# A spectral and GeGLU network in FP32: rows mixed at the loads for a norm, not at residual rows and sequence matrices

## The chip, the cores and the metric

One core of one Trainium2 chip runs the whole program. The time is device microseconds per execution; the profiled execution is one of them, with every instruction and DMA packet recorded. A run of the kernel before took 1851.21 us (median of 3, 1846.16 to 1852.52).

## The reference

Four layers on x of 2048 rows by 512 columns, in FP32: a Fourier mixing layer, a GeGLU layer, and both again, each on the normalised x and added to x.

```python
def _A_ref(x, dft_seq_re, dft_seq_im, dft_hid_re, dft_hid_im):
    a = jnp.einsum("bsd,ed->bse", x, dft_hid_re)
    b = jnp.einsum("bsd,ed->bse", x, dft_hid_im)
    return jnp.einsum("ts,bse->bte", dft_seq_re, a) - jnp.einsum("ts,bse->bte", dft_seq_im, b)

def _B_ref(x, w_gate, w_up, w_down):
    return (_gelu(x @ w_gate) * (x @ w_up)) @ w_down

x = A_x
x = x + _A_ref(_layernorm(x), A_dft_seq_re, A_dft_seq_im, A_dft_hid_re, A_dft_hid_im)
x = x + _B_ref(_layernorm(x), B_w_gate, B_w_up, B_w_down)
```

The two last lines run twice, with the same matrices; the layers are numbered 0 to 3 here.

## The kernel before, in words

**Precision and products.** Every FP32 operand is split into a high part (ACT, `split`, L113) and a low part (DVE, L114), and a product is three matmuls (`mm3`, L147 to L149). Large products are formed by a Strassen-like scheme with seven block products, whose names (A11, A12, S1 to S4, T1 to T4) are those of its blocks and of sums of blocks.

**Tiles.** x stands in DRAM in groups of 512 rows (`xs[layer, g]`, four groups), four tiles of 128 rows in a group. Nearly all tiles in SBUF are 128 by 512 and come from one pool of 98 slots (`sb`, named s). All loads are issued by SP's queue in the order in which they stand; most stores by POOL's.

**Mixing layers (0 and 2, `mix`).** The matrices of the sequence transform (`ws`, 128 tiles of 128 by 512) are loaded as a stream of items (`load_next`, L220), split, and multiplied with the normalised rows; then the matrices of the hidden transform (`wh`) follow. `plan` (L324) gives the order of the steps for the four blocks b: A11 and A12 for the first FORE blocks (four in layer 0, two in layer 2), then for each block S2, S3, A22 and the three groups of the hidden transform. A tile is loaded up to RAW items ahead of its split, and split up to AHEAD items ahead of its use. At the end of a block `x_add` (L175) adds the product to x and stores four tiles. Beside the products a queue of small steps runs, one after each tile's six matmuls (`step`): norms and preparations for what comes.

**GeGLU layers (1 and 3, `geglu`).** A layer is done in two halves (w = 0 and 1) of two parts of 512 rows each. `block_steps` (L502) prepares a half: eight norms (`normed`, L439), each of one tile of 128 rows, each transposed in blocks of 32 by 32 on DVE (L515) into a wide tile; one wide tile of 1 MB for each part goes to DRAM (L518) and comes back in pieces of 32 rows (L529), which completes the transpose. The products with gate, up and down weights (`wb`, `wd`) follow. `load_rows` loads x for the sum and `add_rows` adds and stores.

**What "mixed" is.** The transpose by 32-row blocks leaves the rows of a group in another order: with n the tile, j the block of 32 rows in a tile and t the row in a block, row (n, j, t) stands at place (j, n, t). All products of the layer come out in that order. So before the change tile i of the sum holds 32 rows of each of the four tiles of its group, and x is loaded and stored for it by one transfer of four blocks of 32 rows:

```python
        if mixed:
            return xs[layer, g].rearrange("(n j t) d -> j n t d", n=NT, t=32)[n]
```

The four tiles of the last group of layer 1 stay in SBUF (`fresh`) for layer 2, in mixed order; so in layer 2 the sequence matrices' tiles that meet them, k from 12 to 15 of 16, are put together from four row blocks too (`seq_tile`, L341):

```python
        if layer and k >= NS - NT:
            return ws[(n + 1) * NS - NT:(n + 1) * NS, (k % NT) * 32:(k % NT + 1) * 32]
```

A scheduler that simulates the engines sets the order of instructions on each engine, so an edit in one place moves independent instructions in others.

Of the kernel before, what the change touches and what calls it, by code (L numbers as in the profile page):

```python
# [14 lines left out]
P = 128  # L15
S, D, F = 2048, 512, 1792
NS = S // P
# [4 lines left out]
NT = TB // P  # L22
# [17 lines left out]
def fnet_geglu(ctx: ExitStack, tc: tile.TileContext, x_in, ws, wh, wgu, wdn, out):  # L40
# [27 lines left out]
    nc = tc.nc  # L68
# [37 lines left out]
    sb = Slots(slots, "s", NSLOT)  # L106
# [30 lines left out]
    def plus(out, a, b):  # L137
        nc.vector.tensor_tensor(out, a, b, op=ALU.add)  # L138
# [12 lines left out]
    half = slice(0, 256), slice(256, 512)  # L151

    xg = x_in.rearrange("(g r) d -> g r d", r=TB)
    og = out.rearrange("(g r) d -> g r d", r=TB)
    xs = {(0, g): xg[g] for g in range(NB)}
# [3 lines left out]
    xs.update({(4, g): og[g] for g in range(NB)})  # L161
    fresh = {}

    def rows(layer, i, mixed=False):
        g, n = divmod(i, NT)
        if mixed:
            return xs[layer, g].rearrange("(n j t) d -> j n t d", n=NT, t=32)[n]
        return xs[layer, g][n * P:(n + 1) * P]

    def x_load(layer, i, mixed=False):  # L170
        t = sb.get()
        nc.sync.dma_start(t, rows(layer, i, mixed))
        return t

    def x_add(layer, i, t, ps, mixed=False, keep=False, engine=nc.gpsimd):  # L175

        plus(t, t, ps)
        ps8.put(ps)
        engine.dma_start(rows(layer + 1, i, mixed), t)  # L179
        if keep:  # L180
            fresh[i] = t
        else:
            sb.put(t)
# [81 lines left out]
    def make_a11(k):  # L265

        def run(v):
            held[k] = v
            return split_slot(v)
        return run  # L270
# [42 lines left out]
    def skewed():  # L313

        order = []
        for k in range(NK + SKEW):
            order += [(0, k)] if k < NK else []
            order += [(1, k - SKEW)] if k >= SKEW else []
        return order
# [17 lines left out]
    def bare(layer, b, what):  # L337

        return layer == 0 and b == 0 and what == "A11"

    def seq_tile(layer, n, k):  # L341

        if layer and k >= NS - NT:
            return ws[(n + 1) * NS - NT:(n + 1) * NS, (k % NT) * 32:(k % NT + 1) * 32]
        return ws[n * NS + k]

    def mix_items(layer):
        def raw(make, *tiles):
            items.append((F32, tiles, make, None))

        for b, what in plan(layer):
            tiles = [[seq_tile(layer, b * 2 + m, k) for k in range(NS)] for m in range(2)]
            (a11, a12), (a21, a22) = ((r[:NK], r[NK:]) for r in tiles)
            hold = b >= FORE[layer]
            if what == "A11":
                for k in range(NK):
                    raw(as_is if bare(layer, b, what) else make_a11(k) if hold else plain, a11[k])
            elif what == "A12":
                for t in a12:
                    raw(plain, t)  # L360
            elif what == "S2":
                for second, k in skewed():
                    if second:
                        raw(make_s1(k))
                    else:
                        raw(make_s2(k), a21[k], a22[k], *(() if hold else (a11[k],)))
            elif what == "S3":
                for second, k in skewed():
                    if second:
                        raw(make_s4(k), a12[k])  # L370
                    else:
                        raw(make_s3(k))
            elif what == "A22":
                for t in a22:
                    raw(plain, t)
            else:
                for m, c in what:
                    if layer == 0 and b == 0:
                        items.append((F32, (wh[m * ND + c],), make_hid_first(m, c), (m, c)))
                    else:  # L380
                        items.append((F32R, halves(whs[m, c]), make_hid(m, c), (m, c)))
# [20 lines left out]

    known = {}

    def row_of(layer, i):
        x = fresh.pop(i, None)
        return x_load(layer, i) if x is None else x

# [27 lines left out]
        known[layer, i] = norm_terms(layer, i, x, junk)  # L436
        sb.put(x, junk)

    def normed(layer, i):  # L439
        x = row_of(layer, i)  # L440
        z = sb.get()
        rstd, shift = known.pop((layer, i), None) or norm_terms(layer, i, x, z)
        nc.scalar.activation(z, x, AF.Identity, bias=shift, scale=rstd)  # L443
        sb.put(x)
        return z
# [56 lines left out]
    def block_steps(layer, w):  # L502

        zt, t, wide = {}, {}, {}
        turned = [dram.tile([P, NT * D], F32, name=f"t{layer}_{w}_{part}") for part in range(2)]

        def norm(i):

            def run():
                z = normed(layer, w * 2 * NT + i)  # L510
                part, n = divmod(i, NT)
                if n == 0:
                    wide[part] = tpool.tile([P, NT * D], F32, name="wide")
                to = wide[part].rearrange("p (b n t) -> p b n t", n=NT, t=32)
                nc.vector.transpose(to[:, :, n], z.rearrange("p (b t) -> p b t", t=32))  # L515
                sb.put(z)
                if n == NT - 1:
                    nc.gpsimd.dma_start(turned[part], wide.pop(part))  # L518
            return run

        def fetch(c):

            def run():
                for part in range(2):
                    v = zt[c, part] = sb.get()
                    for i in range(P // 32):
                        cols = turned[part][:, (c * 4 + i) * P:(c * 4 + i + 1) * P]
                        to = v[i * 32:(i + 1) * 32]
                        nc.sync.dma_start(  # L529
                            to.rearrange("p (j t) -> p j t", t=P), cols.rearrange("(j p) t -> p j t", p=32)  # L530
                        )
            return run

        def difference(a, b):
            v = sb.get()
            minus(v, a, b)
            return v

        def first(c):
            def run():  # L540
                v = t[f"B{1 + c // 2}1", c % 2] = zt.pop((c, 0))
                blocks[f"B{1 + c // 2}1", c % 2] = split_slot(v)
            return run

        def second(c):
            def run():
                v = zt.pop((c, 1))
                if c < 2:
                    t["B12", c] = v
                    t["T1", c] = difference(v, t["B11", c])  # L550
                    sb.put(t.pop(("B11", c)))
                else:
                    c0 = c - 2
                    t["T2", c0] = difference(v, t["T1", c0])
                    t["T3", c0] = difference(v, t["B12", c0])
                    sb.put(t.pop(("B12", c0)))
                    blocks["B22", c0] = split_slot(v)
                    sb.put(v)
            return run

        def fourth(c):
            def run():
                t["T4", c] = difference(t["B21", c], t["T2", c])
                sb.put(t.pop(("B21", c)))
            return run

        def divide(name, c):
            def run():
                blocks[name, c] = split_slot(t[name, c])
                sb.put(t.pop((name, c)))  # L570
            return run

        one = [norm(i) for i in range(2 * NT)]
        two = [fetch(c) for c in range(ND)] + [first(c) for c in range(ND)] + [second(c) for c in range(ND)]
        two += [fourth(c) for c in range(2)]
        two += [divide(name, c) for name in ("T2", "T3", "T1", "T4") for c in range(2)]
        return one, two
# [211 lines left out]
    def geglu(w, layer):  # L789

        gs, h, acc = {}, {}, {0: [], 1: []}
# [109 lines left out]
        xrows = []  # L901

        def load_rows(part):
            xrows.extend(x_load(layer, (w * 2 + part) * NT + i, True) for i in range(NT))

        def add_rows(part, keep=False):
            for i in range(NT):
                x_add(layer, (w * 2 + part) * NT + i, xrows.pop(0), acc[part][i], True, keep)

        def last_downs(tail):  # L910

            fs = range(NF - tail, NF)
            vs = [take() for _ in fs]
            for f in fs:
                ready(f, 1)
            for i in range(NT):
                ts = slice(i * P, (i + 1) * P)
                for f, v in zip(fs, vs):
                    hs = h[f, 1]
                    mm3(acc[1][i], (hs[0][:, ts], hs[1][:, ts]), v, f == 0, f == NF - 1)  # L920
                x_add(layer, (w * 2 + 1) * NT + i, xrows.pop(0), acc[1][i], True, engine=nc.sync)

        before_mix = w == 1 and layer < 3
        if before_mix:
# [41 lines left out]
    ps = ps8.get()  # L966
# [81 lines left out]
```

## Time and profile before

| | |
|---|---|
| median of 3 runs | 1851.21 us (1846.16 to 1852.52) |
| profiled execution, its own time | 1846.1 us |
| its span, first to last instruction | 1844.3 us |
| PE busy | 1689.5 us (92%), 7168 matmuls |
| DVE, ACT, POOL busy | 1030.4, 782.1 and 191.9 us |
| DMA | 400.01 MB, mean 217 GB/s |
| mean granted TensorE clock | 0.954 |
| `s<-ws` loads, `s<-x` loads | 432 and 134, 256 KB each |

Busy times of the engines overlap, so they don't add up to the span. PE's busy time holds matmuls at a full and at a reduced clock, so a stretch is better read by the number of matmuls that it got through. The layers follow one another: layer 0 to about 400 us, layer 1 to about 850, layer 2 to about 1350, layer 3 to the end.

### The profile page before, as it was taken

The numbers are of one execution on the slowest core, as the hardware profiler recorded it, in microseconds if no ns is written. First come the engines' busy times: TensorE is split into PE (matmuls) and PEld (weight loads), VectorE is DVE, ScalarE is ACT, GpSimd is POOL, SyncE is SP. The second block draws the span as 40 slices with busy tenths as digits, with TensorE's granted clock in tenths as the row PEclk, the third lists the DMA queues.
The fourth block names the chain that finished last, engine by engine and source line by source line (L and its number), as shares of the span: only waits on it lengthen the run. The fifth ranks groups of instructions, "written<-read, shape, count | busy, mean of one in ns | idle before, by whom it ended". The sixth has DMA issues, their size and how long they took to land.

```text
span 1844.3 us, 22260 instructions
## 1 busy us (share of the span) xinstructions
PE 1689.5 (92%) x7168; PEld 1372.9 (74%) x7168; DVE 1030.4 (56%) x1748; ACT 782.1 (42%) x1504; POOL 191.9 (10%) x344
## 2 busy tenths in 40 slices
PE   9999999999999789999686879779869999979997
PEld 7878888788887568888465667557748888868886
DVE  8997787877664243355574654745752434343340
ACT  8643455455455254345532232543432335433330
POOL 3201011114331110001100000110000000100000
PEclk9999999999999989999788899889979999989999
DMA  9768678798678785576545655457478458785571
GB/s 353 234 212 296 224 239 302 245 329 302 231 249 258 230 289 173 173 239 186 162 150 155 199 157 176 136 168 221 123 222 303 149 181 288 229 285 164 167 233 46
DMA packets 221604, 400.01 MB, mean 217 GB/s; under 512 B 29872, under 2 KB 49840, under 8 KB 220464
## 3 DMA queue, kind: packets, MB, share of 16 engines
q1 hardware_dynamic: 197520, 333.01, 56.6%
q0 software_dynamic: 23968, 65.59, 10.2%
q8 instruction: 56, 0.92, 0.2%
q14 instruction: 60, 0.49, 0.1%
HBM read 331.87 MB, written 66.58 MB: 216 GB/s over the span
## 4 chain that ended last, share of the span: by engine, by line
PE 52%; issue 19%; DMA 17%; DVE 5%; ACT 4%; SPq 1%; POOL 1%; DVEq 0%; ACTq 0%; POOLq 0%
PE p L148 17%; PE p L147 17%; PE p L149 17%; DMA s<-ws 7%; DMA s<-x 5%; DVE s L114 3%; ACT s L113 2%; DMA s<-wd 1%; DMA x<-s 1%; DMA s<-wh 1%; DVE s L135 1%; DVE s L138 1%; ACT s L428 1%; DMA s<-t 1%; SPq L529 1%
## 5 line engine op out<-in xcount | busy, mean ns | idle before, releaser
L147 PE MATMUL p<-s,s 128*128 128x512 f32 x2368 | 919.9, 399 | 109.5 <-ACT s L113 49.6
L148 PE MATMUL p<-s,s 128*128 128x512 f32 x2368 | 940.3, 398 | 33.8 <-DVE s L114 31.2
L149 PE MATMUL p<-s,s 128*128 128x512 f32 x2368 | 924.3, 396 | 0.7 <-DVE s L114 0.7
L113 ACT ACTIVATE s<-s 128x512 fp32r<-128x512 f32 (+1 forms) x782 | 454.6, 617 | 609.8 <-DMA s<-ws 129.4
L114 DVE TENSOR_TENSOR s<-s,s 128x512 fp32r<-128x512 f32 (+1 forms) x782 | 504.2, 675 | 284.3 <-ACT s L113 236.2
L147 PEld LDWEIGHTS p<-s,s 128*128 128x128 f32 x2368 | 454.9, 193 | 217.5 <-ACT s L113 71.9
L148 PEld LDWEIGHTS p<-s,s 128*128 128x128 f32 x2368 | 455.3, 192 | 139.8 <-DVE s L114 41.9
L149 PEld LDWEIGHTS p<-s,s 128*128 128x128 f32 x2368 | 454.0, 192 | 97.2 <-DVE s L114 1.6
L138 DVE TENSOR_TENSOR s<-s,p 128x512 f32<-128x512 f32 x316 | 211.2, 683 | 278.6 <-PE p L149 210.5
L135 DVE TENSOR_TENSOR s<-s,s 128x512 f32<-128x512 f32 (+1 forms) x314 | 185.9, 609 | 90.1 <-DMA s<-ws 42.8
L142 ACT ACTIVATE s<-p 128x512 f32<-128x512 f32 x224 | 129.9, 592 | 161.3 <-PE p L149 153.2
L786 ACT ACTIVATE s<-s 128x512 f32<-128x512 f32 x112 | 70.1, 629 | 122.7 <-DVE s L138 121.8
L138 DVE TENSOR_TENSOR s<-s,s 128x512 f32<-128x512 f32 (+1 forms) x78 | 49.6, 640 | 77.0 <-DMA s<-ws 61.9
L179 POOL DMA_DIRECT2D x<-s x48 | 28.8, 600 | 605.1 <-DVE s L138 604.0
L800 DVE TENSOR_TENSOR s<-s,s 128x512 f32<-128x512 f32 x84 | 57.8, 689 | 2.1 <-ACT s L786 0.3
L429 POOL TENSOR_SCALAR rstd<-rstd 128x1 f32<-128x1 f32 x48 | 14.3, 298 | 425.4 <-ACT s L428 393.6
L443 ACT ACTIVATE s<-s,shift,rstd 128x512 f32<-128x512 f32 x64 | 50.9, 807 | 15.7 <-DMA s<-wd 7.0
L426 ACT ACTIVATE s<-s 128x512 f32<-128x512 f32 x48 | 29.8, 622 | 63.2 <-DMA s<-x 63.1
L207 POOL DMA_DIRECT2D wb<-s x84 | 45.1, 540 | 109.3 <-ACT s L113 88.2
L515 DVE STREAM_TRANSPOSE wide<-s 128x512 f32<-128x512 f32 x32 | 22.2, 704 | 27.7 <-ACT s L443 15.9
L800 DVE TENSOR_TENSOR s<-s,p 128x512 f32<-128x512 f32 x28 | 19.2, 685 | 28.3 <-PE p L149 28.3
L428 ACT ACTIVATE s<-s,mean 128x512 f32<-128x512 f32 x48 | 34.2, 712 | 0.3
(34 smaller groups left out, 244.9 us busy)
## 6 DMA issues: line engine op xcount, KB each, us to landing
s<-ws SPq DMA_DIRECT2D x432, 256.0 KB
s<-wb SPq DMA_DIRECT2D x294, 256.0 KB
s<-wd SPq DMA_DIRECT2D x196, 256.0 KB
s<-x SPq DMA_DIRECT2D x134, 256.0 KB
s<-wh SPq DMA_DIRECT2D x120, 256.0 KB
wb<-s POOLq DMA_DIRECT2D x98, 256.0 KB, 3.8
x<-s POOLq DMA_DIRECT2D x48, 256.0 KB, 6.6
t<-wide POOLq DMA_DIRECT2D x8, 1024.0 KB, 6.8
```

The lines of the kernel that those rows point to most:

```text
L113: nc.scalar.activation(hi, src, AF.Copy)
L114: nc.vector.tensor_tensor(lo, src, f32(hi), op=ALU.subtract)
L135: nc.vector.tensor_tensor(out, a, b, op=ALU.subtract)
L138: nc.vector.tensor_tensor(out, a, b, op=ALU.add)
L142: nc.scalar.activation(v, src, AF.Copy)
L147: nc.tensor.matmul(ps, ah, bh, start=start, stop=False, skip_group_check=True)
L148: nc.tensor.matmul(ps, ah, bl, start=False, stop=False, skip_group_check=True)
L149: nc.tensor.matmul(ps, al, bh, start=False, stop=stop, skip_group_check=True)
L428: nc.scalar.activation(junk, x, AF.Square, bias=mean, accum_out=rstd)
L443: nc.scalar.activation(z, x, AF.Identity, bias=shift, scale=rstd)
L786: nc.scalar.activation(t, g, AF.Gelu_apprx_tanh)
L800: nc.vector.tensor_tensor(t, t, v, op=ALU.mult)
```

## The change

The loads for the norms of the GeGLU layers now take the mixed rows, by four transfers of 32 rows each (`x_load_mixed`), so that the block transpose puts them in their natural order. Everything behind the norm is then in plain order: the residual loads and stores of the GeGLU layers, the fresh tiles, and the sequence matrices' tiles in layer 2. `seq_tile` goes.

```diff
-    def rows(layer, i, mixed=False):
+    def rows(layer, i):
         g, n = divmod(i, NT)
-        if mixed:
-            return xs[layer, g].rearrange("(n j t) d -> j n t d", n=NT, t=32)[n]
         return xs[layer, g][n * P:(n + 1) * P]
...
+    def x_load_mixed(layer, i):
+
+        g, n = divmod(i, NT)
+        t = sb.get()
+        for j in range(NT):
+            r0 = j * P + n * 32
+            nc.sync.dma_start(t[j * 32:(j + 1) * 32], xs[layer, g][r0:r0 + 32])
+        return t
...
-            tiles = [[seq_tile(layer, b * 2 + m, k) for k in range(NS)] for m in range(2)]
+            tiles = [[ws[(b * 2 + m) * NS + k] for k in range(NS)] for m in range(2)]
...
-    def row_of(layer, i):
+    def row_of(layer, i, mixed):
+        if mixed:
+            return x_load_mixed(layer, i)
         x = fresh.pop(i, None)
         return x_load(layer, i) if x is None else x
...
-                z = normed(layer, w * 2 * NT + i)
+                z = normed(layer, w * 2 * NT + i, True)
...
-            xrows.extend(x_load(layer, (w * 2 + part) * NT + i, True) for i in range(NT))
+            xrows.extend(x_load(layer, (w * 2 + part) * NT + i) for i in range(NT))
...
-                x_add(layer, (w * 2 + part) * NT + i, xrows.pop(0), acc[part][i], True, keep)
+                x_add(layer, (w * 2 + part) * NT + i, xrows.pop(0), acc[part][i], keep)
...
-                x_add(layer, (w * 2 + 1) * NT + i, xrows.pop(0), acc[1][i], True, engine=nc.sync)
+                x_add(layer, (w * 2 + 1) * NT + i, xrows.pop(0), acc[1][i], engine=nc.sync)
```

Three places on SP's queue show what moves. A row is a line of the kernel, DMA, the tile written and the tensor read, and the transfer's shape; 128x1x512 is a tile filled from four blocks of 32 rows.

First, layer 2, the last loads of A12 for blocks 0 and 1 and the first of S2. Before:

```order
L220 DMA s_8918<-ws 128x1x512
L220 DMA s_8942<-ws 128x512
L220 DMA s_8960<-ws 128x512
L220 DMA s_8972<-ws 128x512
L220 DMA s_8984<-ws 128x512
L220 DMA s_9008<-ws 128x1x512
L220 DMA s_9020<-ws 128x1x512
L220 DMA s_8906<-ws 128x1x512
L220 DMA s_8890<-ws 128x1x512
L220 DMA s_9032<-ws 128x1x512
L220 DMA s_8930<-ws 128x1x512
L220 DMA s_9044<-ws 128x512
```

Now, at the same place:

```order
L226 DMA s_8966<-ws 128x512
L226 DMA s_8990<-ws 128x512
L226 DMA s_9008<-ws 128x512
L226 DMA s_9020<-ws 128x512
L226 DMA s_9032<-ws 128x512
L226 DMA s_9056<-ws 128x512
L226 DMA s_8938<-ws 128x512
L226 DMA s_9068<-ws 128x512
```

The number and order of the loads are nearly the same, and all have one shape. There are 64 such four-block loads of `ws` in layer 2.

Second, layer 0, block 2, where the norms of layer 1 begin. Before:

```order
L172 DMA s_2862<-x_0_85 128x512
L220 DMA s_2880<-ws 128x512
L220 DMA s_2882<-ws 128x512
L172 DMA s_2907<-x_0_85 128x512
L220 DMA s_2922<-ws 128x512
L220 DMA s_2924<-ws 128x512
L172 DMA s_2951<-x_0_85 128x512
L172 DMA s_2989<-x_0_85 128x512
```

Now:

```order
L178 DMA s_2862<-x_0_85 32x512 x4
L226 DMA s_2883<-ws 128x512
L226 DMA s_2885<-ws 128x512
L178 DMA s_2910<-x_0_85 32x512 x4
L226 DMA s_2928<-ws 128x512
L226 DMA s_2930<-ws 128x512
L178 DMA s_2957<-x_0_85 32x512 x4
L226 DMA s_2932<-ws 128x512
L178 DMA s_2998<-x_0_85 32x512 x4
```

Each norm's load has become four entries, ahead of the same `ws` loads.

Third, the end of the program. Before, the last residual load and the four stores of the last tiles:

```order
L172 DMA s_16040<-x_3_96 128x1x512
L179 DMA out<-s_16040 4x32x512
L179 DMA out<-s_16042 4x32x512
L179 DMA out<-s_16044 4x32x512
L179 DMA out<-s_16046 4x32x512
```

Now:

```order
L169 DMA s_16136<-x_3_96 128x512
L185 DMA out<-s_16136 128x512
L185 DMA out<-s_16138 128x512
L185 DMA out<-s_16140 128x512
L185 DMA out<-s_16142 128x512
```

The order is the same; the four stores have lost their four-block shape.

## Rows read from the trace of the kernel before

**Rows 1.** The page, part 1: busy time of PE, share of span.
```profile
PE 1689.5 (92%) x7168; PEld 1372.9 (74%) x7168; DVE 1030.4 (56%) x1748; ACT 782.1 (42%) x1504; POOL 191.9 (10%) x344
```
**Rows 2.** Windows: stretch, then busy us and instructions of each engine.
```profile
core 0: us, PE busy (x) PEld busy (x) DVE busy (x) ACT busy (x) POOL busy (x), PEclk, DMA share, GB/s
...
50.00:350.00 300.00, 296.05 (x1295) 243.32 (x1294) 251.46 (x425) 143.40 (x272) 37.22 (x61) 0.99 0.76 255
350.00:400.00 50.00, 45.27 (x185) 36.13 (x184) 45.44 (x77) 26.18 (x47) 2.64 (x6) 0.93 0.79 251
...
600.00:700.00 100.00, 80.63 (x325) 64.25 (x324) 37.98 (x60) 41.65 (x93) 12.25 (x25) 0.90 0.79 250
...
850.00:1350.00 500.00, 407.84 (x1642) 324.34 (x1641) 298.10 (x491) 200.90 (x396) 29.96 (x53) 0.90 0.54 164
1350.00:1400.00 50.00, 37.01 (x149) 29.93 (x147) 17.98 (x30) 12.04 (x22) 0.00 (x0) 0.82 0.87 297
1400.00:1600.00 200.00, 200.00 (x884) 165.67 (x883) 75.11 (x115) 81.14 (x162) 12.52 (x26) 1.00 0.68 223
1600.00:1650.00 50.00, 40.16 (x159) 32.16 (x158) 23.16 (x36) 16.61 (x28) 2.85 (x4) 0.90 0.75 224
```
**Rows 3.** Waits of PE, 850 to 1400 us: total, times, longest.
```profile
PE p L147 <- ACT s L113: 35.2, 10, 7.8
PE p L147 <- DVE s L138: 28.5, 2, 14.8
PE p L148 <- DVE s L114: 28.0, 12, 6.7
PE p L147 <- DMA s<-wh: 13.0, 1, 13.0
```
**Rows 4.** Waits of ACT and DVE for ws loads, 50 to 350 us (layer 0).
```profile
ACT s L113 <- DMA s<-ws: 13.6, 13, 2.4
...
DVE s L138 <- DMA s<-ws: 19.8, 9, 3.9
...
DVE s L135 <- DMA s<-ws: 6.9, 8, 1.7
```
**Rows 5.** Waits of ACT and DVE for ws loads, 850 to 1400 us (layer 2).
```profile
ACT s L113 <- DMA s<-ws: 112.8, 31, 9.8
...
DVE s L138 <- DMA s<-ws: 42.1, 11, 8.0
DVE s L135 <- DMA s<-ws: 35.9, 18, 3.7
```
**Rows 6.** Pieces of the chain that ended last: start us, us, what.
```profile
250.24 4.68 DMA s<-x
...
313.97 3.96 DMA s<-ws
...
645.66 2.15 DMA s<-t
...
1092.26 14.69 DMA s<-ws
...
1289.86 10.42 DMA s<-ws
...
1344.92 13.61 DMA s<-wh
...
1612.61 17.37 DMA s<-x
```
**Rows 7.** By tile, SP's issues: duration ns min/median/max, first and last start.
```profile
L220 SPq DMA_DIRECT2D s<-ws x432: 322/374/4064, 1.2 to 1346.5; - x144
...
L529 SPq DMA_DIRECT2D s<-t x128: 302/430/1785, 353.5 to 1610.3; - x128
```
**Rows 8.** SP at the end: its stores by timeline, and its last wait.
```profile
1827.34 8.70 SPq L179 DMA_DIRECT2D out<-s  x4
...
SPq L1044 <- DMA out<-s: 6.9, 3, 3.4
```

More of the change, by code (lines that the diff above doesn't have):

```diff
@@ L162, in fnet_geglu, with x_load, x_add @@
     fresh = {}
-    def rows(layer, i, mixed=False):
+    def rows(layer, i):
         g, n = divmod(i, NT)
-        if mixed:
-            return xs[layer, g].rearrange("(n j t) d -> j n t d", n=NT, t=32)[n]
         return xs[layer, g][n * P:(n + 1) * P]
-    def x_load(layer, i, mixed=False):
+    def x_load(layer, i):
         t = sb.get()
-        nc.sync.dma_start(t, rows(layer, i, mixed))
+        nc.sync.dma_start(t, rows(layer, i))
         return t
-    def x_add(layer, i, t, ps, mixed=False, keep=False, engine=nc.gpsimd):
+    def x_load_mixed(layer, i):
[5 more added lines that the diff above has]
+        return t
+    def x_add(layer, i, t, ps, keep=False, engine=nc.gpsimd):
         plus(t, t, ps)
         ps8.put(ps)
-        engine.dma_start(rows(layer + 1, i, mixed), t)
+        engine.dma_start(rows(layer + 1, i), t)
         if keep:
@@ L339, in bare @@
         return layer == 0 and b == 0 and what == "A11"
[L341 to L345, printed above, removed]
     def mix_items(layer):
@@ L437, in terms_ahead, with normed @@
         sb.put(x, junk)
-    def normed(layer, i):
-        x = row_of(layer, i)
+    def normed(layer, i, mixed=False):
+        x = row_of(layer, i, mixed)
         z = sb.get()
```

## The prediction

> **What bounds the kernel now.** I read the busy times first, then the stretches, then who PE waited for, then who those engines waited for, and last the chain. PE is busy for 92% of the span [rows 1], so it is the bound on average; what can be gained is read from the stretches in which it is not. A stretch is best read by its matmuls. From 1400 to 1600 us PE does 884 in 200 us, 0.2262 us each, with the clock granted in full [rows 2]. Layer 0 from 50 to 350 us does 1295 in 300 us, 0.2317 us each: nearly the same pace. Layer 2 has the same work but does 1642 in 500 us and 149 in the next 50 [rows 2]. At 0.2262 us these 1791 matmuls would take 405 us, so 145 of 550 us are lost there, more than anywhere else. Of these, 105 us are waits of PE for ACT's and DVE's splits and sums and one `wh` load [rows 3], and the other 40 are matmuls at a lower clock: the granted share is 0.90 and 0.82 there against 0.99 in layer 0 [rows 2], part of it at the lower of TensorE's levels (1.2 GHz in place of 2.4), which it falls to after PE has stood still.
>
> Why do ACT and DVE come late? In layer 0 ACT waits 13.6 us in total for `ws` loads, never over 2.4, and DVE 26.7 [rows 4]. In layer 2 ACT waits 112.8 us for them, up to 9.8 at a time, and DVE 78.0 [rows 5]. Yet the DMA engines are less used there: a share of 0.54 and 164 GB/s, against 0.76 and 255 in layer 0 [rows 2]. So it is not the total traffic. In the chain a `ws` load of layer 0 stands with 3.96 us, loads of layer 2 with 10.42 and 14.69, and a `wh` load behind them with 13.61 [rows 6]; SP itself takes up to 4064 ns to issue one `ws` load where the median is 374 [rows 7]. What differs between the layers in these loads is the shape: 64 of layer 2's are put together from four blocks of 32 rows. A load of this shape is slow while the mean DMA share is low, as if few engines carried it, and plain loads issued behind it are slow too.
>
> The Trainium skill has a rule for this (DMA: Bandwidth & Descriptors, "Why a DMA increments its semaphore by 16 and not by 1"): a transfer runs on the largest number of engines up to 16 that divides the outermost sizes of both sides, which is four for four blocks against 128 partitions. By it the change puts these loads on all 16 engines and the sum is the one below; without it the rows only say that this shape and the lateness go together, and the second rival would deserve more. The low share in rows 2 agrees; no row counts engines.
>
> **The change part by part.** The sum is made against the profiled execution, 1846.1 us (span 1844.3 and 1.8 around it); the median of the runs is 5 us above it.
>
> *Sequence matrices, layer 2.* The same 64 loads become plain; nothing else moves on that queue but neighbours that change places. At layer 0's pace 1791 matmuls take 415 us. Both ends of the layer, where the norms before and the weights behind fall in, get what the end of layer 0 lost beyond that pace: 50 us for 185 matmuls, 7.1 us over [rows 2], twice. That makes 429 in place of 550: a gain of 121 us. Bounds: 145 at the pace of rows 2's best stretch; below, no gain at all if the shape is not the cause. I take layer 0 because it is the same code with plain loads, and more loads in the same time (255 GB/s).
>
> *Residual rows of the GeGLU layers.* 32 loads and 32 stores become plain. In the change of halves of layer 3 the chain holds one such load of 17.37 us [rows 6], and 1600 to 1650 us does 159 matmuls, worth 36.0 us: 14.0 lost [rows 2]. I take 10 of them, between 0 and 14. In layer 1 the same place, 600 to 700 us, does 325, worth 73.5: 26.5 lost [rows 2]. But weights are also being made and stored there and all loads crowd, so I take 5, between -8 (the crowd only shifts) and 26.5.
>
> *The last four stores.* They are on the path: the first is issued at 1827.34 us and the fourth 8.70 us later, at about 1836, and SP then waits for their landing [rows 8] until 1844.3. A plain load in a busy stretch lands in about 4 to 5 us [rows 6], so 4 of these 8 us go; between 0 and 6.9.
>
> *Norm loads.* 32 tiles have four entries on SP's queue in place of one. Nearest is the fetch of a transposed piece, also 32 rows: 430 ns an issue against 374 for a plain load [rows 7]. That is 4 times 430 less 374, 1.35 us more for each tile and 43 us of queue in all, ahead of `ws`, `wh`, `wd` and `wb` loads that stand behind them on SP, and ACT waits for four landings. These norms are queued well ahead of their use, and layer 0, where eight of them are made, has waits for `ws` of at most 3.9 us [rows 4]; so the loads that run ahead of PE cover most. Cost between 0 and 43; I take 8, about a fifth, because the cover is thinnest only at the changes of halves. If the cover is gone, the next thing late is the split of the next `ws` tile. The reads now need all four stores of a group instead of one; the group is stored a whole step of the plan earlier, so I cost this at nothing, and what covers it is the block of products in between (if it were late, one landing of 4 to 5 us each half).
>
> Sum: 1846.1 - 121 - 10 - 5 - 4 + 8 = 1714.1 in the profiled execution's terms; the runs lie 0 to 6 above that, so I say **1717 us**.
>
> **The rivals.**
>
> *Layer 2 is also held by something else.* Its plan is not layer 0's: only two blocks have their first half done ahead, so later blocks load, sum and split within the block. For it: PE's longest waits are for DVE sums (14.8 us) and not all of the waits in rows 3 end in a load. Against it: DVE is busy 298 of 500 us there and 251 of 300 in layer 0 [rows 2], so it has room. If half of the 121 stays, the time is 1717 + 60 = 1777.
>
> *The four-block shape is not the cause.* Then layer 2 keeps its 145 us, and what is left is 10 + 5 + 4 - 8 = 11 us: 1838. Were the norm loads also to cost 30 instead of 8, there would be no change. Against it stands the contrast of rows 4 and 5.
>
> *Slower: the pieces serialize.* If the four pieces of a norm's tile land one behind the other, and everything behind them on SP's queue waits with them, each tile costs three more landings. The shortest piece of 32 rows in the chain took 2.15 us [rows 6], so 32 tiles cost 32 x 3 x 2.15 = 206 us if nothing covers it, and with none of the gain in layer 2 this ends at 2050; with it, at about 1717 - 8 + 206 = 1915. It decides from 4.5 us uncovered for each tile, where it eats the 140 us of gain. Against it: 128 such pieces are fetched already, and PE loses 7.1 us where 32 of them go at 350 to 400 us [rows 2]. The Trainium skill speaks for this rival (DMA: Bandwidth & Descriptors, "Rules for kernel authors"): it advises against splitting a tile by partitions, since the parts share the same engines and gain nothing, and wants one transfer of 128 partitions. The rows agree that a piece costs an issue as long as a whole tile's.
>
> **How the numbers follow.** Forecast 0.71; layer 2 held by something else 0.20; shape not the cause 0.05; pieces serialize 0.04. A measurement of this kernel can tell about 0.3% (5.5 us) from no change. Faster 0.94: the first two, and 0.03 of the third; same 0.02, the rest of the third; slower 0.04. The forecast alone, with its bounds, runs from about 1685 to 1760. The range goes on to 1790 to take in the first rival, and leaves the other two and the extreme ends of the bounds out.
>
> **What would show it.** Right: 850 us onward runs at 0.23 to 0.24 us a matmul, the granted clock near 0.98, DMA share near 0.75; ACT's waits for `ws` in layer 2 fall from 112.8 to under 30 us; SP's longest `ws` issue is about 1.5 us; the last store lands within 5 us. Wrong: ACT still waits 60 us or more for `ws` there; or waits for x by the norms (L426, L443) grow by tens of us; or PE waits for transposed pieces at the changes of halves.

## The result and the profile after

The kernel after takes 1695.05 us (median of 4, 1693.33 to 1699.06) against 1851.87 for the kernel before in the same comparison (1846.16 to 1854.31). The ratio is 0.916, with an interval from 0.9132 to 0.9188. The profiled execution has a span of 1691.4 us in place of 1844.3, so 152.9 us have gone.

The page of the kernel after, part 1, with busy time, share of the span and instructions:

```profile
span 1691.4 us, 22376 instructions
PE 1649.1 (98%) x7168; PEld 1350.6 (80%) x7168; DVE 1029.7 (61%) x1748; ACT 784.6 (46%) x1504; POOL 186.1 (11%) x344
```

DVE and ACT do the same work as in [rows 1]; PE is now busy for 98% of the span. PE's busy time fell by 40 us with as many matmuls, because more of them ran at the higher of the clock's two levels: the mean granted share rose from 0.954 to 0.993.

The windows of the kernel after, columns as in [rows 2]. Layer 2 now stands at about 850 to 1250 us:

```profile
50.00:350.00 300.00, 293.52 (x1281) 240.75 (x1280) 248.97 (x420) 142.18 (x270) 35.58 (x59) 0.99 0.76 252
...
600.00:700.00 100.00, 92.04 (x384) 74.66 (x383) 39.31 (x62) 47.52 (x106) 10.70 (x25) 0.95 0.79 260
...
850.00:1250.00 400.00, 388.02 (x1690) 316.92 (x1690) 297.11 (x486) 197.38 (x376) 25.50 (x46) 1.00 0.68 223
```

Layer 2 does 1690 matmuls in 400 us, 0.237 us each, where it did 1642 in 500 [rows 2]. The DMA share rose from 0.54 to 0.68 and the rate from 164 to 223 GB/s: nearly the same bytes in less time. The change of halves of layer 1 does 384 in 100 us in place of 325. Layer 0 is a little slower, 1281 in place of 1295.

The waits of ACT and DVE for `ws` loads in layer 2, 850 to 1245 us, as in [rows 5], and below them all of PE's waits there, as in [rows 3]:

```profile
ACT s L113 <- DMA s<-ws: 21.1, 14, 2.6
...
DVE s L138 <- DMA s<-ws: 16.1, 7, 4.1
...
DVE s L135 <- DMA s<-ws: 6.5, 11, 1.5
```

```profile
PE p L147 <- DMA s<-wh: 4.8, 1, 4.8
PE p L147 <- ACT s L113: 3.6, 3, 1.7
PE p L148 <- DVE s L114: 3.6, 4, 1.5
```

ACT's 112.8 us are 21.1, DVE's 78.0 are 22.6, and PE's 105 us are 12. Where the time went along the program can be read by setting the start of the same matmul, by its count from the first, beside each other in the two traces:

| Matmul number | Place | Before, us | After, us | Difference |
|---|---|---|---|---|
| 1800 | layer 1 begins | 430.2 | 432.6 | +2.4 |
| 2600 | layer 1, before the change of halves | 613.0 | 613.9 | +0.9 |
| 3600 | end of layer 1 | 866.6 | 854.1 | -12.4 |
| 5200 | end of layer 2 | 1374.2 | 1234.1 | -140.0 |
| 6200 | layer 3, change of halves | 1600.8 | 1466.2 | -134.7 |
| 7167 | last matmul | 1834.4 | 1687.1 | -147.3 |

The last 5.6 us lie behind the last matmul: 9.6 us from its end to the span's end before, 3.9 after.

The list of DMA issues of the kernel after, the last number being the median of the us from issue to landing:

```profile
s<-ws SPq DMA_DIRECT2D x432, 256.0 KB, 3.9
...
s<-x SPq DMA_DIRECT2D x102, 256.0 KB, 4.2
...
x<-s POOLq DMA_DIRECT2D x48, 256.0 KB, 4.8
s<-x SPq DMA_DIRECT2D x128, 64.0 KB, 3.6
...
out<-s POOLq DMA_DIRECT2D x12, 256.0 KB, 6.2
...
out<-s SPq DMA_DIRECT2D x4, 256.0 KB, 2.0
```

In the same list of the kernel before, SP's lines have no landing at all, and the stores stand with more:

```profile
s<-ws SPq DMA_DIRECT2D x432, 256.0 KB
...
x<-s POOLq DMA_DIRECT2D x48, 256.0 KB, 6.6
...
out<-s POOLq DMA_DIRECT2D x12, 256.0 KB, 10.3
```

The missing number goes with the shape of the loads. The profile pairs issues and landings only where each transfer leaves 16 completion events on its semaphore. Counted from the trace's semaphore events, a plain load leaves 16, and a load of four blocks that SP issues leaves 5. POOL's stores leave 16 in either shape, so for them the count tells nothing. The runs below show what the count of SP's loads goes with.

SP's own waits for the landing of `ws` loads, which the prediction did not read, show in the same windows. First before (850 to 1400 us), then after (850 to 1245 us):

```profile
SPq L220 <- DMA s<-ws: 52.9, 25, 5.1
```

```profile
SPq L226 <- DMA s<-ws: 2.9, 6, 1.4
```

SP's transfers take turns on eight semaphores, and in the traces of before, after, `e2`, `e3` and `e6` none starts before the one eight places ahead of it has landed; so at most eight are in flight, and a load that lands late also holds back the issue of what stands behind it. This is one way in which lateness and a low DMA share can go together.

### The profile page after: what moved, and what is told of

Same layout as the page of the kernel before. It is cut to its first block, busy times and chain, and to the rows that moved or that the text cites. A ratio compares the mean times of both kernels' runs of the same rounds, so it can differ in the third digit from the quotient of the medians.

```text
span 1691.4 us, 22376 instructions
## 1 busy us (share of the span) xinstructions
PE 1649.1 (98%) x7168; PEld 1350.6 (80%) x7168; DVE 1029.7 (61%) x1748; ACT 784.6 (46%) x1504; POOL 186.1 (11%) x344
## 4 chain that ended last, share of the span: by engine, by line
PE 76%; DMA 9%; DVE 6%; ACT 4%; issue 2%; SPq 2%; POOL 1%; DVEq 0%; ACTq 0%; POOLq 0%
PE p L148 25%; PE p L149 25%; PE p L147 25%; DVE s L114 3%; DMA s<-x 3%; DMA s<-ws 2%; DVE s L135 2%; ACT s L113 2%; DMA s<-wd 1%; SPq L531 1%; DVE s L138 1%; DMA s<-wb 1%; ACT s L445 1%; ACT s L430 1%; ACT s L428 1%
## 5 line engine op out<-in xcount | busy, mean ns | idle before, releaser
L148 PE MATMUL p<-s,s 128*128 128x512 f32 x2368 | 925.6, 391 | 6.4 <-DVE s L114 6.4
L147 PE MATMUL p<-s,s 128*128 128x512 f32 x2368 | 904.5, 393 | 26.5 <-DVE s L138 7.9
L149 PE MATMUL p<-s,s 128*128 128x512 f32 x2368 | 911.8, 391 | 3.5 <-DVE s L114 3.5
L147 PEld LDWEIGHTS p<-s,s 128*128 128x128 f32 x2368 | 446.7, 189 | 127.0 <-ACT s L113 20.7
L148 PEld LDWEIGHTS p<-s,s 128*128 128x128 f32 x2368 | 447.3, 189 | 103.7 <-DVE s L114 10.6
L149 PEld LDWEIGHTS p<-s,s 128*128 128x128 f32 x2368 | 447.0, 189 | 97.7 <-DVE s L114 3.9
```

Source lines behind the costliest of these rows:

```text
L147: nc.tensor.matmul(ps, ah, bh, start=start, stop=False, skip_group_check=True)
L148: nc.tensor.matmul(ps, ah, bl, start=False, stop=False, skip_group_check=True)
L149: nc.tensor.matmul(ps, al, bh, start=False, stop=stop, skip_group_check=True)
```

## The experiments

The theory to test: a transfer whose outermost count is four runs on four DMA engines; it lands late, and what is issued behind it on these engines lands late too. The rivals: layer 2 gains from something else that the plain order brings (stores, schedule); the scatter of rows in DRAM or the split by partitions is what is slow; the four pieces cost more than they save. All ratios are to the kernel before on the same chip. The kernel after, in its own comparison, has 0.916.

**One part alone.** `e1_ws_plain` is the kernel before with this edit:

```diff
-        if layer and k >= NS - NT:
-            return ws[(n + 1) * NS - NT:(n + 1) * NS, (k % NT) * 32:(k % NT + 1) * 32]
         return ws[n * NS + k]
```

> The kernel before, with the 64 four-block loads of the sequence matrices in layer 2 made plain and nothing else (rows of the last group then meet the wrong columns, so layer 2 computes something else at the same cost). If the shape of these loads holds layer 2, it gains what layer 2 gained in the whole change, 127 us: about 1724 us, a ratio of 0.931, with the change of halves in layer 1 and the end as before. If layer 2 gained from the plain order of x, from its stores or from another order of the schedule: under 60 us of gain, 1790 us or more.

It took 1730.15 us, ratio 0.9362 (0.9334 to 0.9391); the span is 1726.4 us, 117.9 below the kernel before. So the shape of 64 loads is worth about 118 us, three quarters of the whole. The first rival falls. The 6 us that are missing to the forecast are not lost in layer 2: by the matmul count, layer 2 gains 122 us, and the change of halves of layer 1, which the edit does not touch, loses 6. ACT's waits for `ws` in layer 2 (850 to 1255 us) show it:

```profile
ACT s L113 <- DMA s<-ws: 25.0, 15, 6.5
```

**The same rows by four transfers.** `e2_ws_pieces` is also the kernel before, reading the same addresses into the same places:

```diff
-            stream["last"] = nc.sync.dma_start(t if dtype == F32 else f32(t), a)
+            if isinstance(a, list):
+                for j, piece in enumerate(a):
+                    stream["last"] = nc.sync.dma_start(t[j * 32:(j + 1) * 32], piece)
+            else:
+                stream["last"] = nc.sync.dma_start(t if dtype == F32 else f32(t), a)
...
-            return ws[(n + 1) * NS - NT:(n + 1) * NS, (k % NT) * 32:(k % NT + 1) * 32]
+            return [ws[(n + 1) * NS - NT + j, (k % NT) * 32:(k % NT + 1) * 32] for j in range(NT)]
```

> The kernel before, with the same 64 tiles read from the same addresses into the same places, but each by four transfers of 32 rows in place of one transfer of four blocks; 192 more entries on SP's queue. If what is slow is the one transfer of four blocks (few engines carry it), most of the 127 us come back: 1725 to 1750 us. If it is the place of the rows in DRAM or the split by partitions that is slow, layer 2 stays as it was or gets worse: 1846 us or more. If pieces are a little worse than plain, the difference to the run with plain loads prices a piece.

It took 1729.2 us, ratio 0.9355 (0.9329 to 0.938), the same as with plain loads, with ACT waiting as little (850 to 1255 us):

```profile
ACT s L113 <- DMA s<-ws: 26.2, 17, 5.1
```

Neither the place of the rows nor the split by partitions is slow; the one transfer of four blocks is. And 192 more entries on SP's queue cost nothing that can be measured here.

**The same part put back.** `e3_ws_blocks` is the kernel after with `seq_tile` as it was before.

> The kernel after, with the four-block loads of the sequence matrices put back in layer 2 alone (it computes something else there). If the shape is the cause in both surroundings, layer 2 loses 120 to 130 us again: 1815 to 1825 us. If the plain residual rows and stores have opened room, it loses clearly less, say 60: 1755 us.

It took 1805.69 us, ratio 0.9768 (0.9743 to 0.9793), 110.9 us of span above the kernel after, all of it between the same two matmuls of layer 2 as above. That is 9 us under the forecast of 120 to 130, but far from the 60 of the rival. ACT in layer 2 (850 to 1355 us) and SP's issues of `ws` (ns min/median/max):

```profile
ACT s L113 <- DMA s<-ws: 104.3, 27, 9.9
```

```profile
L226 SPq DMA_DIRECT2D s<-ws x432: 323/367/3170, 1.2 to 1317.7; - x144
```

The long issues come back with the shape: 3170 ns, where the kernel after has at most 1720.

**Is it the count of blocks?** Two kernels put the 64 loads together from 16 and from 8 blocks, so that the outermost count differs (and with it the number of tiles in DRAM that a load's rows come from). `e9_ws_16`, on the kernel after (`e10_ws_8` has 8 and 16 where this has 16 and 8):

```diff
+    def seq_tile(layer, n, k):
+        if layer and k >= NS - NT:
+            return ws[(n + 1) * NS - 16:(n + 1) * NS, (k % NT) * 8:(k % NT + 1) * 8]
+        return ws[n * NS + k]
...
-            tiles = [[ws[(b * 2 + m) * NS + k] for k in range(NS)] for m in range(2)]
+            tiles = [[seq_tile(layer, b * 2 + m, k) for k in range(NS)] for m in range(2)]
```

> The kernel after, with the same 64 loads of the sequence matrices in layer 2 as one transfer of 16 blocks of 8 rows, from 16 tiles in place of one (other values, the same bytes and rows of 2 KB). If four blocks were slow because the outermost count sets how many DMA engines carry a transfer, 16 blocks are as good as plain: within 5 us of after, 1695 us, where four blocks cost 111. If it is the scatter over several tiles in DRAM or the blocked shape as such, it is slow again: 1780 us or more.

> As the run before, with 8 blocks of 16 rows. By the count of engines a load carries twice what a plain one does per engine and half of what four blocks do; queueing makes it less than half as bad: 5 to 50 us slower than after, 1700 to 1745 us. If shape as such is slow: as four blocks, 1805 us.

With 16 blocks: 1692.06 us, ratio 0.9179 (0.9157 to 0.9202), no different from the kernel after. With 8: 1726.5 us, 0.9361 (0.9338 to 0.9385). In span against the kernel after:

| Blocks of a load | Span above after, us | Completion events of a load | Median landing of these loads in layer 2, us |
|---|---|---|---|
| 16 | -1.0 | 16 | 3.1 to 3.4, 5.1 at its end |
| 8 | +30.3 | 9 | 4.5 to 5.3, 8.6 at its end |
| 4 | +110.9 | 5 | 6.2 to 12.3 |

The last two columns are worked out from the semaphore events in the traces; a landing counts from the end of the load's issue, and the medians are of stretches of 100 us. ACT's waits in layer 2 follow, first with 16 blocks (850 to 1245 us), then with 8 (850 to 1275 us):

```profile
ACT s L113 <- DMA s<-ws: 35.0, 23, 3.4
```

```profile
ACT s L113 <- DMA s<-ws: 54.7, 23, 4.6
```

So it is the count, not the blocked shape. The Trainium skill states this rule (DMA: Bandwidth & Descriptors, "Why a DMA increments its semaphore by 16 and not by 1"): a transfer uses the largest number of engines up to 16 that divides the outermost sizes, each engine adds one to the semaphore, and the issuing queue adds the rest at once. The events agree with it: 4 + 1, 8 + 1 and 16. No trace names the engine that moved a packet, so that four and eight engines carry these loads rests on this rule and on the events.

**The pieces against one transfer of four blocks.** `e4_norm_one` changes the norm loads of the kernel after:

```diff
-        for j in range(NT):
-            r0 = j * P + n * 32
-            nc.sync.dma_start(t[j * 32:(j + 1) * 32], xs[layer, g][r0:r0 + 32])
+        nc.sync.dma_start(t, xs[layer, g].rearrange("(j n t) d -> n j t d", n=NT, t=32)[n])
```

> The kernel after, with each mixed norm load as one transfer of four blocks (the same rows in the same places, 96 entries fewer on SP's queue). By the theory the 32 loads are slow and hold up what is issued behind them, but they run ahead of their use: 3 to 25 us slower than after, 1698 to 1720 us. If the four entries on the queue are what costs, it is faster than after by up to 10 us: 1685 us.

Both forecasts missed: 1741.6 us, ratio 0.9417 (0.9395 to 0.944), 46.8 us of span above the kernel after. The loads run ahead of their use, but not by enough. In the chain (start us, us) they stand with up to 14.10 us, and a `wh` load behind two of them with 9.68:

```profile
254.66 8.60 DMA s<-x
...
269.95 9.68 DMA s<-wh
...
292.03 11.32 DMA s<-x
...
585.14 13.26 DMA s<-x
...
1477.47 14.10 DMA s<-x
```

This place shows how the lateness spreads. Two `ws` loads issued at 260.5 and 264.4 us land after 3.2 and 2.6 us; the two four-block loads follow at 264.9 and 265.5, and the six plain loads of `ws` and `wh` issued from 266.1 to 270.4 us land after 9.7 to 11.2.

**What the pieces still cost.** `e5_norm_plain` loads a plain tile at the same place:

```diff
-        for j in range(NT):
-            r0 = j * P + n * 32
-            nc.sync.dma_start(t[j * 32:(j + 1) * 32], xs[layer, g][r0:r0 + 32])
+        nc.sync.dma_start(t, xs[layer, g][n * P:(n + 1) * P])
```

> The kernel after, with each norm load as one plain transfer of 128 rows (the rows come out in the wrong order, so it computes something else at the same cost). This is the price of the four pieces: layer 0 fell behind by 2.4 us in the change and the change of halves in layer 3 by 5.3 before it won 12.6. If the pieces cost that, 3 to 8 us faster than after: about 1689 us. If they are covered, the same within 2 us; if the pieces clog the queue (the rival), 20 us faster or more.

It took 1680.58 us, ratio 0.9098 (0.9065 to 0.9131), 15.4 us of span below the kernel after: more than forecast, less than the rival's bound. By the two ratios it is 11 us, and each ratio is sure to 5 or 6 us only. By the matmul count, 5 us of it lie in layer 0 where the norms of layer 1 are made, 3 in the change of halves of layer 1, 3 in layer 2 and 7 in the change of halves of layer 3 (3 us of layer 0 go the other way earlier, before any norm load differs, so that pieces of 3 us are no larger than what else moves). The last place shows in the windows, 1400 to 1500 us, first of the kernel after, then of this one:

```profile
1400.00:1500.00 100.00, 95.09 (x411) 77.94 (x411) 47.07 (x74) 48.33 (x108) 11.84 (x26) 0.98 0.88 294
```

```profile
1400.00:1500.00 100.00, 100.00 (x442) 82.65 (x442) 49.80 (x78) 51.38 (x112) 11.84 (x26) 1.00 0.89 313
```

In the kernel after ACT's norms wait there for x, and with plain norm loads they do not:

```profile
ACT s L428 <- DMA s<-x: 11.0, 2, 9.4
```

**Residual loads and stores.** `e6_res_blocks` loads the residual rows by the old four-block pattern, `e7_store_blocks` stores by it from POOL, `e8_last_blocks` does so for the last four stores alone. The edits in part; the last line is that of `e7` and `e8`, which pass `blocks=True` where they call it:

```diff
+    def blocks_of(layer, i):
+        g, n = divmod(i, NT)
+        return xs[layer, g].rearrange("(n j t) d -> j n t d", n=NT, t=32)[n]
...
+    def x_load_blocks(layer, i):
+        t = sb.get()
+        nc.sync.dma_start(t, blocks_of(layer, i))
...
-            xrows.extend(x_load(layer, (w * 2 + part) * NT + i) for i in range(NT))
+            xrows.extend(x_load_blocks(layer, (w * 2 + part) * NT + i) for i in range(NT))
...
-        engine.dma_start(rows(layer + 1, i), t)
+        engine.dma_start(blocks_of(layer + 1, i) if blocks else rows(layer + 1, i), t)
```

> The kernel after, with the residual loads of the GeGLU layers as one transfer of four blocks each (other rows are added, at the same cost). If these 32 loads are what the changes of halves gained by, they give back 10 to 22 us: 1705 to 1717 us, at 600 to 700 us in layer 1 and at the same place in layer 3. If the stores or the order gave the gain: within 3 us of after.

> The kernel after, with the stores of the GeGLU layers that POOL issues as transfers of four blocks (rows land in other places, at the same cost). They landed after a median of 8 us in layer 1 before and land after about 5 now. If slow stores hold up loads beside them, 3 to 12 us are given back, in the changes of halves: 1698 to 1707 us. If a store that nobody waits for costs nothing: within 2 us of after.

> The kernel after, with the last four stores alone as transfers of four blocks (rows land in other places). They are on the path, and the span behind the last matmul was 9.6 us before and is 3.9 now: 5 to 6 us slower than after, 1700 us, all of it behind the last matmul.

The loads cost more than their forecast: 1724.73 us, ratio 0.9332 (0.9306 to 0.9358), 30.7 us of span. By the matmul count, 15 us go in layer 1 at the change of halves, 6 at the start of layer 2 and 9 at the change of halves of layer 3. The stores too: 1716.69 us, 0.9282 (0.9248 to 0.9315), 23.4 us, of which 8 in the change of halves of layer 1 and 11 at the start of layer 2. The last four stores: 1698.49 us, 0.919 (0.9163 to 0.9217), an interval that overlaps with that of the kernel after; in the profiled executions the span is 5.4 us longer, and all of it lies behind the last matmul, 9.7 us in place of 3.9. Here the shape can be seen without a crowd: the first of the four stores, with nothing else in flight, lands 6.0 us after its issue with four blocks and 2.0 us plain.

What waits in the change of halves of layer 1 (600 to 700 us) is PE, for splits that wait for pieces of the transpose. First the kernel after, then with residual loads in blocks, then with stores in blocks:

```profile
PE p L147 <- ACT s L113: 2.2, 2, 1.4
```

```profile
PE p L147 <- ACT s L113: 12.9, 2, 12.6
```

```profile
PE p L147 <- ACT s L113: 8.8, 2, 8.4
```

The pieces come late in two ways. With residual loads in blocks, these are issued at 622 to 627 us and land at 633 to 643, and SP issues the second batch of pieces from 643.5 us on, where the kernel after does so from 625.5. With stores in blocks, the first of them goes out at 602.7 us on POOL's queue; pieces issued on SP's before it land after 3.0 to 3.4 us, those issued from 603.4 to 606.6 after 6.6 to 12.0. In the chains, a residual load stands with 16.29 us in the first of these two kernels, and a piece of the transpose with 11.02 and a store with 13.44 in the second:

```profile
624.21 16.29 DMA s<-x
```

```profile
606.61 11.02 DMA s<-t
...
827.76 13.44 DMA x<-s
```

And SP's last wait, first of the kernel after, then with the last four stores in blocks, as in [rows 8]:

```profile
SPq L1046 <- DMA out<-s: 1.4, 1, 1.4
```

```profile
SPq L1050 <- DMA out<-s: 7.0, 3, 3.4
```

**A version that was to beat both.** If plain norm loads are worth 15 us, x could be stored twice by the mixing layers, the second time in the order that the norms want. `e11_two_stores` does it by four stores of 32 rows, `e12_two_stores_blocks` by one of four blocks; both load the norms' rows from this second copy, `xm`:

```diff
-        for j in range(NT):
-            r0 = j * P + n * 32
-            nc.sync.dma_start(t[j * 32:(j + 1) * 32], xs[layer, g][r0:r0 + 32])
+        nc.sync.dma_start(t, xm[layer, g][n * P:(n + 1) * P])
...
         engine.dma_start(rows(layer + 1, i), t)
+        if layer % 2 == 0:
+            g, j = divmod(i, NT)
+            for n in range(NT):
+                r0 = n * P + j * 32
+                engine.dma_start(xm[layer + 1, g][r0:r0 + 32], t[n * 32:(n + 1) * 32])
```

> The kernel after, but the mixing layers store x twice, plain and, by four stores of 32 rows on POOL's queue, in the order that the norms want; so each norm load is one plain transfer again. Plain norm loads were worth 14.5 us; the 128 more stores of 64 KB each run where POOL has time. 5 to 14 us faster than after: about 1685 us. If the stores crowd the DMA engines or hold POOL's steps of the norms (rstd): the same as after, or up to 15 us slower.

> As the run before, with the second store as one transfer of four blocks on POOL's queue, 32 in place of 128. Such stores in the GeGLU layers cost 22 us for 28 of them. If they are slow wherever they run, it is 5 us or more slower than with four stores of 32 rows; if only the changes of halves are tight, it is as good: about 1685 us.

Both miss: 1721.25 us, ratio 0.9338 (0.9314 to 0.9361), and 1730.43 us, 0.9374 (0.934 to 0.9407); 26.1 and 36.6 us of span above the kernel after. The gain at the change of halves of layer 3 is there (7 us in both, by the matmul count), but in the first 14 us go in layer 0, most of them around the second block's products, and 23 in layer 2; in the second it is 24 and 23. In the trace of the first, PE's waits for ACT's and DVE's splits are 22.5 and 24.6 us over the whole run, against 7.0 and 6.4 in the kernel after; two of them, 1.1 and 4.7 us, end when a second store lands, since the slot that the split writes was that store's source. The others end in work of DVE and ACT that this study did not follow further, so what else the second store costs stays open. The order is as the second forecast has it, by 9 us of the medians, though the intervals overlap: with four blocks, the store lands after a median of 12.2 us against 4.2 for a piece.

## Why the prediction was right, and where its sizes were off

The likeliest case came true: 1695.05 us, within the range of 1685 to 1790, and 22 us under the 1717 forecast. The sum took off 132 us, the spans differ by 152.9. Term by term, with what the experiments give:

| Term | Forecast, us | Measured, us | From |
|---|---|---|---|
| `ws` loads in layer 2 | -121 | -118 and -111 | `e1`, `e3` |
| residual loads | -15, loads and stores together | -30.7 | `e6` |
| stores from POOL | in the 15 above | -23.4 | `e7` |
| last four stores | -4 | -5.4 | `e8` |
| norm loads | +8 | +15.4 | `e5` |
| sum | -132 | -155 with 111 | span: -152.9 |

The terms measured against the kernel after, each put back alone, add up to the whole within about 2 us, so little is left for other causes; with `e1`'s 118 the sum is -162, 9 us over. The total came closer than its terms, and that is partly luck: residual rows and stores were 39 us short, while `ws` and the norm loads were 17 us too hopeful.

*Sequence matrices.* Right in mechanism and size. The step that carried it was to take the layer's pace from layer 0, which has the same code with plain loads, and not from an engine's total. That 128 us lie between the ends of layers 1 and 2 in the first table is because some of the gain of the plain residual rows and stores falls there, 16 us by `e6` and `e7`.

*Residual rows and stores.* The mechanism was right, the size was not: "I take 10 of them" and "I take 5" were sized by what two changes of halves lost before, for all 64 transfers, and came to 15 where 54 were measured (45 by what `e1` leaves of the whole: 152.9 less 117.9 is 35.0, to which the norm loads' 15.4 come and from which the last stores' 5.4 go). What failed is the place. For the change of halves of layer 3 the 10 were right, 9 by `e6` and 2 by `e7`. The step left out the start of layer 2, where the residual loads and stores of layer 1's last tiles cost 16 us together; and for layer 1, where 15 and 8 us were measured in place of 5, it put most of the loss down to the crowd of weights. About half of that loss went with the change: 600 to 700 us lost 13 us in place of 26.5 (384 matmuls by 0.2262 are 86.9 us).

*Norm loads.* Also under-sized, 15.4 in place of 8. "The loads that run ahead of PE cover most" holds for the queue entries (192 more cost nothing in `e2`), but the norms themselves are on the path at the changes of halves. Why a piece costs more there than a plain load is not shown; four pieces take four of the eight places that SP has for loads in flight, but no run tries this apart. The rival in which pieces serialize asked for 206 us and does not hold. The Trainium skill's advice behind it (DMA: Bandwidth & Descriptors, "Rules for kernel authors"), one transfer of 128 partitions in place of parts, is right for the norm loads where that transfer can be plain: 15 us (for the 64 `ws` loads of `e2` the parts cost nothing). Where it would have four blocks, the parts win by 47 us (`e4`).

*The end.* The four stores gave 5.4 us, the forecast was 4: it took the landing of a plain load in a busy stretch, 4 to 5 us, and at the end a plain store lands after 2.0.

Of the signs that the prediction named, the pace (0.237), the clock, ACT's 21.1 us, SP's longest issue (1.72 us) and the landing of the last store (2.0 us) came out; the DMA share rose to 0.68, not 0.75. Of the signs of being wrong none came: the waits of the norms for x fell from 66.5 to 53.8 us over the run.

The rival in which layer 2 is held by something else for half of its gain is out: PE waits 12 us there in all.

## What to carry to other kernels

When loads come late while the DMA engines' mean share is low, look at the outermost count of the transfers: one of few blocks lands late even by itself (6.0 us in place of 2.0 here), and what is issued behind it lands late as well. Cut such a transfer into parts whose outermost count has 16 as a divisor, or move the reordering to where the fewest and least urgent transfers bear it; here 32 reordered loads took the place of 128 reordered transfers. Price it from a stretch with the same code and plain transfers, and look for its cost at each place where transfers crowd, not only at those that the chain shows.

## What was not expected

A transfer of four blocks costs out of proportion: with 8 blocks 64 loads cost 30 us, with 4 blocks 111. Half as many blocks is nearly four times the time. The granted clock goes down with it: a mean share of 0.991 over the run with 16 blocks, 0.985 with 8 and 0.962 with 4. PE's busy time, with the same matmuls, is 10 us above that of the kernel after with 8 blocks and 29 with 4 (1659.4 and 1678.3 against 1649.1); that much of the 30 and 111 us are slower matmuls, the rest is idle time.

Stores that nobody waits for directly cost 23 us when they went out in four blocks. The twelve to `out` have a median landing of 9.1 us with blocks and 6.2 without; by the chain, what comes late is a piece of the transpose and a slot.
